# Shift columns in three loads, a quarter of the scale columns accumulated on VectorE, and the last q tile from shifted k-tiles

## Chip, cores, metric

One core of one Trainium2 chip. The metric is device microseconds of one execution. The kernel before takes about 831 us.

## The reference, cut to what matters

A transformer block: a conditioned layer norm, linear attention, a second conditioned layer norm and a gated feed-forward. Only the first projection matters here. The conditioning vector `c` gives one scale (`ca`) and one shift (`sa`) per column; `x` has 2048 rows of 1024 columns.

```python
mod = (_silu(c) @ w_mod).reshape(c.shape[0], 6, 1, -1)
sa, ca, ga, sb, cb, gb = (...)                      # 1024 columns each
h = _layernorm(x, axis=-1) * (1 + ca) + sa
x = x + ga * _A_ref(h, A_wqkv, A_wo)                # q, k, v = h @ wqkv ; linear attention ; @ wo
# [... second half cut ...]
```

## The kernel before

Rows come in four chunks of 512. The first chunk's q projection runs while the weights of scale and shift still arrive. Scale and shift are therefore computed in pieces, each just ahead of the k-tile (128 columns of `h`) that needs it. One piece of 128 columns is eight matmuls with one output column ("products"), into bank 0 of PSUM, the memory that TensorE writes (the program divides it into eight banks):

```python
def mod_sc(w, c0, ms):                       # scale (WCA, c0=8) or shift (WSA, c0=0) columns of the tiles ms
    for m in ms:
        for kt in range(NDT):
            P.pe("matmul", out=PS[:, 0, c0 + m:c0 + m + 1], lhsT=w[:, kt, m * 128:(m + 1) * 128],
                 rhs=SILUC[:, kt:kt + 1], ...)
def fin_ca(m, n):                            # VectorE: 1 + scale, out of bank 0
def fin_sa(m, n, cast=False):                # VectorE: shift, out of bank 0, in float32 and as bf16
```

K-tiles 6 and 7 get scale and shift before use. K-tiles 0 to 5 are used scaled only, and their shift is added to q as a bias, `wq.T @ shift` (`bias_mm`, one-column matmuls again). Seven q tiles accumulate at once in seven banks, k-tile by k-tile; the eighth follows in bank 0. The program orders its work by banks: its recorder of operations makes an access of one engine to a bank wait for the last access of any other engine to it (one such wait is the 0.35 us at 22.30 in the profile after, below).

```python
for nt in range(7):
    if nt == 3:
        mod_sc(WCA, 8, range(4, 8)); fin_ca(4, 4)
        for dt in (4, 5): h0_scale_only(dt)            # VectorE
    q_part(nt, qb[nt], (2, 3))
act_stats(4)
for nt in range(7):
    if nt == 4:
        mod_sc(WSA, 0, range(6, 8)); fin_sa(6, 2)      # needs shift columns 768-1023
        for dt in (6, 7): h0_scale(dt)                 # VectorE, scale and shift
    q_part(nt, qb[nt], (4, 5))
mod_sc(WSA, 0, range(4, 6)); fin_sa(4, 2, True)
for nt in range(7):
    if nt == 2: bias_mm((4, 5))
    q_part(nt, qb[nt], (6,))
for nt in range(7):
    if nt == 1:
        mod_sc(WSA, 0, range(4)); fin_sa(0, 4, True)   # needs shift columns 0-511
        # [... statistics of x tile 5 ...]
    if nt == 4: bias_mm(range(4)); bias_fin()
    q_part(nt, qb[nt], (7,))
# [... eighth q tile in bank 0, then exp and relu of all q tiles, then k of chunk 0 ...]
```

The shift columns come in two loads of 512 columns: 512-1023 ahead of the last two weight tiles, 0-511 behind them.

Of the kernel before, what the change touches and what calls it, by code (L numbers as in the profile page):

```python
# [6 lines left out]
BF16 = mybir.dt.bfloat16  # L7
U8 = mybir.dt.uint8
ACT = mybir.ActivationFunctionType
ALU = mybir.AluOpType  # L10
# [252 lines left out]
def bass_adaLN_cond__linear_attn_block__swiglu_ffn__prompt_kernel(  # L263
# [17 lines left out]
    NDT = D // 128  # L281
# [4 lines left out]
    with ExitStack() as es:  # L286
# [6 lines left out]
        def T(name, off, shape, dt):  # L293
            n = 1
            for s_ in shape[1:]:
                n *= s_
            assert off % 32 == 0 and off + n * mybir.dt.size(dt) <= ARENA, (name, off, shape)
            return nc.alloc_sbuf_tensor_at(name, shape, dt, offset=base + off)
# [3 lines left out]
        PQT = T("pqt", 32 * KB, [128, NHG, S], BF16)  # L302
        WCA = T("wca", 32 * KB, [128, NDT, D], BF16)
        WSA = T("wsa", 48 * KB, [128, NDT, D], BF16)
        AT = T("at", 72 * KB, [128, NFT, 512], BF16)
        SM = 64 * KB
# [7 lines left out]
        MODCOL = T("modcol", SM + 1120, [128, 4, NDT], FP32)  # L314
# [13 lines left out]
        ZCOL = T("zcol", SM + 2304, [128, NHG], FP32)  # L328
        RED = T("red", SM + 2336, [128, NDT], FP32)
        MASK4 = T("mask4", SM + 2368, [128, 4], BF16)  # L330
        BIASQ = T("biasq", SM + 2784, [128, NDT], FP32)
        SUMXH = T("sumxh", SM + 2816, [128, NST, 2], FP32)
        NMR = T("nmr", SM + 2944, [128, NST], FP32)
# [5 lines left out]
        HT = T("ht", 120 * KB, [128, 2, NDT, 512], BF16)  # L339
# [7 lines left out]
        ACC = T("acc", 192 * KB, [128, D], FP32)  # L347
        MHL = T("mhl", 196 * KB, [128, 2, D], BF16)
# [7 lines left out]
        SILUF = T("siluf", SM + 7744, [128, NDT], FP32)  # L356
# [22 lines left out]
        PS = nc.alloc_psum_tensor("ps", [128, 8, 512], FP32)  # L379
# [12 lines left out]
        wmv = w_mod.rearrange("(kt p) n -> p kt n", p=128)  # L392
        cv8 = c.rearrange("o (kt p) -> (o kt) p", p=128)

        P = _Prog()
# [5 lines left out]
        def ca_load(p):  # L401
            P.dma("wca%d" % p, WCA[:, :, 512 * p:512 * p + 512], wmv[:, :, D + 512 * p:D + 512 * p + 512])

        def sa_load(p):
            P.dma("wsa%d" % p, WSA[:, :, 512 * p:512 * p + 512], wmv[:, :, 512 * p:512 * p + 512])

        def wq_load(i, n=1):
            P.dma("wq%d" % i, WQK[:, i:i + n, 0:D], wqkvv[:, i:i + n, 0:D])
# [3 lines left out]
        wq_load(2, 2)  # L412
        ca_load(1)
        wq_load(4, 2)
        sa_load(1)
        wq_load(6)
        wq_load(7)
        sa_load(0)
        for j in range(2):
            P.dma("x1_%d" % j, XRES[:, 4 + j, :], xv[:, 4 + j, :])  # L420
        for i in (1, 0):
# [21 lines left out]
        P.dve("memset", ap=MASK[:], constant=0.0)  # L443
        for h in range(4):
            P.dve("memset", ap=MASK[32 * h:32 * h + 32, 32 * h:32 * h + 32], constant=1.0)
        P.dve("memset", ap=MASK4[:], constant=0.0)
        for h in range(4):
            P.dve("memset", ap=MASK4[32 * h:32 * h + 32, h:h + 1], constant=1.0)
        P.dve("memset", ap=ZSEL[:], constant=0.0)
# [54 lines left out]
        def mod_sc(w, c0, ms):  # L504
# [3 lines that stand above are left out]
                         rhs=SILUC[:, kt:kt + 1], start=mod_first[0], stop=(kt == NDT - 1), skip_group_check=True)  # L508
                    mod_first[0] = False

        def fin_ca(m, n):
            P.dve("tensor_scalar", out=MODCOL[:, 0, m:m + n], in0=PS[:, 0, 8 + m:8 + m + n], scalar1=1.0, scalar2=None,
                  op0=ALU.add)

        def fin_sa(m, n, cast=False):
            if cast:
                P.dve("tensor_copy", out=MODTMP[:, m:m + n], in_=PS[:, 0, m:m + n])
            P.dve("tensor_copy", out=MODCOL[:, 1, m:m + n], in_=PS[:, 0, m:m + n])

        def h0_scale_only(dt):  # L520
            P.dve("tensor_scalar", out=HT[:, 0, dt, :], in0=HT[:, 1, dt, :], scalar1=MODCOL[:, 0, dt:dt + 1],
                  scalar2=None, op0=ALU.mult)

        def h0_shift(dt):
            P.dve("tensor_scalar", out=HT[:, 0, dt, :], in0=HT[:, 0, dt, :], scalar1=MODCOL[:, 1, dt:dt + 1],
                  scalar2=None, op0=ALU.add)

        def bias_mm(dts):
            for nt in range(NDT):
                for dt in dts:  # L530
                    P.pe("matmul", out=PS[:, 0, 16 + nt:17 + nt], lhsT=WQK[:, dt, nt * 128:(nt + 1) * 128],
                         rhs=MODTMP[:, dt:dt + 1], start=False, stop=(dt == 3), skip_group_check=True)

        def bias_fin():
            P.dve("tensor_copy", out=BIASQ[:], in_=PS[:, 0, 16:24])

        def t_view(dt, n=1):
            return PSB[:, 4 + dt // 2, (dt % 2) * 512:(dt % 2 + n) * 512]
# [112 lines left out]
        def phi_evac(bank, dst, bias=0.0):  # L651
            i = phi_ctr[0] % 4
            phi_ctr[0] += 1
            P.act("activation", out=E1[:, i, :], in_=PS[:, bank, :], func=ACT.Exp, bias=bias)
            if not isinstance(dst, tuple):
                P.act("activation", out=RL[:, i, :], in_=PS[:, bank, :], func=ACT.Relu, bias=bias)
            phi_pend.append((i, dst, bank))
            if len(phi_pend) == 2:
                phi_flush()
# [22 lines left out]
        def q_part(nt, bank, dts):  # L682
            for dt in dts:
                P.pe("matmul", out=PS[:, bank, :], lhsT=WQK[:, dt, nt * 128:(nt + 1) * 128],
                     rhs=HT[:, 0, dt, :], start=(dt == 0), stop=(dt == 7))
# [56 lines left out]
        def q_phase_chunk0(side):  # L742
            qb = [1, 2, 3, 4, 6, 7, 5]
            fin_ca(2, 2)
            for dt in (2, 3):
                h0_first(dt, "dve")
            for nts, dts in ((range(4), (0,)), (range(4), (1,)), ((4, 5, 6), (0, 1))):
                for nt in nts:
                    q_part(nt, qb[nt], dts)
            for nt in range(7):  # L750
                if nt == 3:
                    mod_sc(WCA, 8, range(4, 8))
                    fin_ca(4, 4)
                    for dt in (4, 5):
                        h0_scale_only(dt)
                q_part(nt, qb[nt], (2, 3))
            act_stats(4)
            for nt in range(7):
                if nt == 4:
                    mod_sc(WSA, 0, range(6, 8))  # L760
                    fin_sa(6, 2)
                    for dt in (6, 7):
                        h0_scale(dt)
                q_part(nt, qb[nt], (4, 5))
            mod_sc(WSA, 0, range(4, 6))
            fin_sa(4, 2, True)
            for nt in range(7):
                if nt == 2:
                    bias_mm((4, 5))
                q_part(nt, qb[nt], (6,))  # L770
            for nt in range(7):
                if nt == 1:
                    mod_sc(WSA, 0, range(4))
                    fin_sa(0, 4, True)
                    ln_ops[1][0]()
                    ln_ops[1][1]()
                if nt == 4:
                    bias_mm(range(4))
                    bias_fin()
                q_part(nt, qb[nt], (7,))  # L780
            ln_ops[1][2]()
            ln1_rstd1(5)
            for f in act_mv_ops(4):
                f()
            neg_rstd(4)
            q_phi = lambda nt: phi_evac(qb[nt] if nt < 7 else 0, PQT[:, nt, 0:512], bias=BIASQ[:, nt:nt + 1])
            for i, dt in enumerate((4, 5, 0, 1, 2, 3, 6, 7)):
                P.pe("matmul", out=PS[:, 0, :], lhsT=WQK[:, dt, 896:1024], rhs=HT[:, 0, dt, :], start=(i == 0),
                     stop=(i == 7))
            for dt in (4, 5):  # L790
                h0_shift(dt)
            ln1_xn(5)
            th_dma(5)
            for dt in range(4):
                h0_shift(dt)
            ln1_xn(4)
            th_dma(4)
            for nt in range(8):
                q_phi(nt)
                for f in side.get(nt, []):  # L800
                    f()
            qk_ctr[0] = 0
# [5 lines left out]
        ln_ops = [ln1_stats_ops(4 + jj) for jj in range(4)]  # L808
# [291 lines left out]
        for ch in range(NCH):  # L1100
            nxt = ch + 1 if ch + 1 < NCH else None
            for ft in range(NFT):
# [4 lines left out]
                for dt in range(NDT):  # L1107
                    P.pe("matmul", out=PS[:, gbank, :], lhsT=GUG[slot][:, dt, ftl * 128:(ftl + 1) * 128],
                         rhs=H2T[:, dt, :], start=(dt == 0), stop=(dt == NDT - 1))
                for dt in range(NDT):  # L1110
                    P.pe("matmul", out=PS[:, ubank, :], lhsT=GUU[slot][:, dt, ftl * 128:(ftl + 1) * 128],
                         rhs=H2T[:, dt, :], start=(dt == 0), stop=(dt == NDT - 1))
# [4 lines left out]
                if ch == 0 and ft % 2 == 0 and ft < 14:  # L1117
                    i = ft // 2
# [11 lines left out]
                if nxt is None and ft in (8, 12):  # L1130
# [3 lines left out]
                          in1=GB_B[:, 896:1024].unsqueeze(1).to_broadcast([128, f1 - f0, 128]), op=ALU.mult)  # L1134
# [5 lines left out]
            for j in range(4):  # L1140
# [3 lines left out]
                if not last:  # L1144
                    for ft in range(NFT):
                        for nh in range(2):
                            P.pe("matmul", out=PS[:, bb + nh, :], lhsT=AT[:, ft, j * 128:(j + 1) * 128],
                                 rhs=WD(ft)[:, nh * 512:nh * 512 + 512], start=(ft == 0), stop=(ft == NFT - 1))
                for nh in range(2):
                    i = nh  # L1150
                    parts = [(0, 384, bb + 1), (384, 512, 4)] if last and nh == 1 else [(0, 512, bb + nh)]
                    for (c0, c1, pb) in parts:
                        if last:
                            for ft in range(NFT):
                                P.pe("matmul", out=PS[:, pb, c0:c1], lhsT=AT[:, ft, j * 128:(j + 1) * 128],
                                     rhs=WDG[:, ft, :] if c0 > 0 else WD(ft)[:, nh * 512 + c0:nh * 512 + c1],
                                     start=(ft == 0), stop=(ft == NFT - 1))
# [46 lines left out]
```

## Time and profile before

| | before |
|---|---|
| median of the first 3 runs, us | 830.80 (830.74 to 831.32) |
| profiled span, us | 829.4 |
| TensorE busy | 99% of the span |

These lines are from the page of the kernel before: the span, busy time, and the chain of work that ended last, by engine and by line. (All operations are recorded through one helper, hence one line number.)

```profile
span 829.4 us, 10017 instructions
...
PE 823.2 (99%) x4083; PEld 378.8 (46%) x4083; DVE 312.6 (38%) x665; ACT 197.5 (24%) x336; POOL 39.9 (5%) x57
...
PE 97%; DMA 2%; SPq 1%; issue 0%; DVE 0%
PE ps L176 97%; DMA wsa<-in_w_mod_dram 2%; SPq L176 1%; DVE xres L176 0%
```

TensorE bounds the kernel. The chain ends in a load, `wsa`, the shift columns.

This is the TensorE timeline, before: start, length, engine, operation, output<-inputs, count, and in brackets idle time and what ended it. `wca` are products for the scale, `wsa` for the shift, `modtmp` for the bias.

```profile
10.28 0.54 PE L176 MATMUL ps<-siluc,wca 128*128 128x1 bf16 x16
...
16.29 0.94 PE L176 MATMUL ps<-siluc,wca 128*128 128x1 bf16 x32
17.09 3.61 PE L176 MATMUL ps<-ht,wqk 128*128 128x512 bf16 x16
20.93 0.55 PE L176 MATMUL ps<-siluc,wsa 128*128 128x1 bf16 x16 [0.23 <-DMA wsa<-in_w_mod_dram]
21.34 1.46 PE L176 MATMUL ps<-ht,wqk 128*128 128x512 bf16 x6
...
25.30 0.95 PE L176 MATMUL ps<-siluc,wsa 128*128 128x1 bf16 x32
...
26.75 0.94 PE L176 MATMUL ps<-modtmp,wqk 128*128 128x1 bf16 x32
27.56 2.75 PE L176 MATMUL ps<-ht,wqk 128*128 128x512 bf16 x12
```

Two marks are used from here on. **P** is the start of the first scale product (10.28 here). **E** is the end of the last bias product (27.56, where the next matmul starts; some matmul records are missing from a trace, and where that one is, E is the start of the last bias products plus the 0.70 us that 28 of them take elsewhere). From E to the end of the span TensorE hardly waits: 829.4 - 27.56 = 801.8 us, and that remainder was within 0.1 us of 801.8 in 12 of the 18 traces of this study. So the stage from P to E is where the change acts, and its length was 17.28 us.

The weight-load side of TensorE, in the view of waits restricted to 10 to 30 us:

```profile
PEld ps L176 <- DMA wsa<-in_w_mod_dram: 1.1, 2, 0.7
```

(Total, times, longest, in us. Weight loads run ahead of the matmuls, so they show a wait as longer than the array loses by it: the longest here is 0.7, and the array's own wait at 20.93 is 0.23.)

### The profile page before, as it was taken

How to read it: one execution, taken by the hardware profiler on the slowest of the kernel's cores; microseconds unless marked ns; L12 is line 12 of the kernel's file. 1: busy time of each engine (PE TensorE's matmuls, PEld its weight loads, DVE VectorE, ACT ScalarE, POOL GpSimd, SP SyncE). 2: the span in 40 equal slices, each digit the busy share in tenths (PEclk: the TensorE clock that was granted, in tenths of full speed). 3: DMA queues.
4: the chain of work that ended last, by engine and by line, in shares of the span. 5: the costliest groups of instructions: out<-in, count | busy, mean ns of one | idle time of the engine just before them, and what ended most of it. 6: DMA issues, size and time to landing. Idle time of an engine off the chain costs nothing.

```text
span 829.4 us, 10017 instructions
## 1 busy us (share of the span) xinstructions
PE 823.2 (99%) x4083; PEld 378.8 (46%) x4083; DVE 312.6 (38%) x665; ACT 197.5 (24%) x336; POOL 39.9 (5%) x57
## 2 busy tenths in 40 slices
PE   8999999999999999999999999999999999999998
PEld 4544444444444444444444444444444444444444
DVE  5797986756955521121221112122111211221111
ACT  4757641323242111011111101111110111111011
POOL 1010000000130000030000003000000300000000
PEclk9999999999999999999999999999999999999999
DMA  9969656938397985700455571045557004553000
GB/s 321 287 151 231 148 159 171 201 104 304 60 256 229 276 264 158 192 25 15 124 155 150 153 185 33 16 124 153 154 151 190 26 18 123 154 152 87 0 26 26
DMA packets 199246, 119.28 MB, mean 144 GB/s; under 512 B 57881, under 2 KB 182945, under 8 KB 199201
## 3 DMA queue, kind: packets, MB, share of 16 engines
q1 hardware_dynamic: 199184, 118.65, 52.8%
q8 instruction: 32, 0.52, 0.3%
q14 instruction: 14, 0.11, 0.0%
q10 hardware_dynamic: 16, 0.00, 0.0%
HBM read 100.67 MB, written 4.33 MB: 127 GB/s over the span
## 4 chain that ended last, share of the span: by engine, by line
PE 97%; DMA 2%; SPq 1%; issue 0%; DVE 0%
PE ps L176 97%; DMA wsa<-in_w_mod_dram 2%; SPq L176 1%; DVE xres L176 0%
## 5 line engine op out<-in xcount | busy, mean ns | idle before, releaser
L176 PE MATMUL ps<-h2t,gug 128*128 128x512 bf16 x896 | 211.7, 379 | 0.0
L176 PE MATMUL ps<-h2t,guu 128*128 128x512 bf16 x896 | 211.7, 379 | 0.0
L176 DVE TENSOR_TENSOR at<-sg,ps 128x512 bf16<-128x512 bf16 x112 | 77.0, 687 | 282.8 <-PE ps L176 281.2
L176 ACT ACTIVATE sg<-ps 128x512 bf16<-128x512 f32 x112 | 66.9, 597 | 309.7 <-PE ps L176 309.7
L176 PEld LDWEIGHTS ps<-h2t,guu 128*128 128x128 bf16 x896 | 87.6, 98 | 105.7
L176 PEld LDWEIGHTS ps<-h2t,gug 128*128 128x128 bf16 x896 | 87.7, 98 | 105.5
L176 PE MATMUL ps<-wd_a,at 128*128 128x512 bf16 (+1 forms) x512 | 112.4, 377 | 0.0
L176 PE MATMUL ps<-ht,wqk 128*128 128x512 bf16 x512 | 111.7, 379 | 0.0
L176 PE MATMUL ps<-wd_b,at 128*128 128x512 bf16 (+1 forms) x384 | 85.0, 377 | 0.0
L176 PEld LDWEIGHTS ps<-wd_a,at 128*128 128x128 bf16 x512 | 50.1, 98 | 59.6
L176 DVE TENSOR_TENSOR ut<-att,gb_b 128x512 bf16<-128x512 bf16 (+1 forms) x32 | 14.3, 447 | 166.8 <-ACT att L176 166.8
L176 PEld LDWEIGHTS ps<-ht,wqk 128*128 128x128 bf16 x512 | 49.5, 98 | 58.7 <-DVE biasq L176 0.2
L176 ACT ACTIVATE att<-ps 128x512 bf16<-128x512 f32 (+1 forms) x32 | 17.4, 591 | 182.1 <-PE ps L176 182.1
L176 PEld LDWEIGHTS ps<-wd_b,at 128*128 128x128 bf16 x384 | 37.6, 98 | 44.7
L176 PE MATMUL ps<-pk,xres 128*128 128x512 bf16 x256 | 56.5, 379 | 0.0
L176 PE MATMUL ps<-mw,pqt 128*128 128x512 bf16 x256 | 56.3, 379 | 0.0
L176 POOL TENSOR_SCALAR h2t<-h2t,modcol 128x512 bf16<-128x512 bf16 x32 | 26.3, 836 | 383.4 <-DMA h2t<-xn 383.4
L176 ACT ACTIVATE e<-ps 128x512 bf16<-128x512 f32 x56 | 33.1, 603 | 31.7 <-PE ps L176 19.8
L176 PEld LDWEIGHTS ps<-mw,pqt 128*128 128x128 bf16 x256 | 24.9, 98 | 30.2 <-DVE xres L176 0.4
L176 PEld LDWEIGHTS ps<-pk,xres 128*128 128x128 bf16 x256 | 24.9, 98 | 29.9 <-issue 0.4
L176 ACT ACTIVATE junk<-xres 128x1024 bf16<-128x1024 bf16 x24 | 25.4, 1058 | 35.1 <-DVE xres L176 34.9
L176 DVE SCALAR_TENSOR_TENSOR xres<-ps,xres 128x512 bf16<-128x512 f32 x32 | 21.4, 688 | 12.3 <-PE ps L176 11.5
(107 smaller groups left out, 344.8 us busy)
## 6 DMA issues: line engine op xcount, KB each, us to landing
gug<-in_B_w_gate_dram SPq DMA_DIRECT2D x56, 512.0 KB, 4.0
guu<-in_B_w_up_dram SPq DMA_DIRECT2D x56, 512.0 KB, 5.3
xres<-in_A_x_dram SPq DMA_DIRECT2D x20, 256.0 KB, 7.7
rb<-recip_den SPq DMA_DIRECT2D x8, 512.0 KB, 11.5
stgx<-in_w_mod_dram SPq DMA_DIRECT2D x2, 2048.0 KB, 7.9
wd_a<-in_B_w_down_dram SPq DMA_DIRECT2D x4, 1024.0 KB, 7.8
out_dram<-xres SPq DMA_DIRECT2D x31, 128.0 KB, 1.7
xres<-in_A_x_dram SPq DMA_DIRECT2D x3, 1024.0 KB, 14.1
```

The source lines that it names most:

```text
L176: return getattr(e, method)(**kw)
```

## The change

Its intent is to take one-column matmuls off TensorE and to have the shift columns for tiles 6 and 7 earlier:

- the shift load of columns 512-1023 is cut in two, and 768-1023 goes first;
- the scale columns 768-1023 are no longer 16 products: VectorE multiplies and adds the eight k-tiles, splits the float32 sum into two bf16 parts, and 4 products with a column of ones add over the partitions;
- the scalings of k-tiles 4 and 5 go to ScalarE, to free VectorE for that;
- k-tiles 0 to 5 are shifted early, so the eighth q tile needs no bias (7 bias columns instead of 8), and the statistics of x tile 5 go behind the shifts.

```diff
-        sa_load(1)
+        sa_load(768, 1024)
         wq_load(6)
         wq_load(7)
-        sa_load(0)
+        sa_load(512, 768)
+        sa_load(0, 512)
@@
+        def part_macc_ops(w, c0, n):          # [... cut: 2 multiplies, 6 multiply-adds in two accumulators ...]
+            ops.append(lambda: P.dve("tensor_tensor", out=acc[0], in0=acc[0], in1=acc[1], op=ALU.add))
+            ops.append(lambda: P.dve("tensor_copy", out=MHL[:, 0, c0:c0 + n], in_=acc[0]))
+            ops.append(lambda: P.dve("tensor_tensor", out=MHL[:, 1, c0:c0 + n], in0=acc[0], in1=MHL[:, 0, c0:c0 + n],
+                                     op=ALU.subtract))
+        def part_sum(c0, ms):                 # [... 2 products per tile, with ONESC ...]
@@ h0_scale_only
-            P.dve("tensor_scalar", out=HT[:, 0, dt, :], in0=HT[:, 1, dt, :], scalar1=MODCOL[:, 0, dt:dt + 1], ...)
+            P.act("activation", out=HT[:, 0, dt, :], in_=HT[:, 1, dt, :], func=ACT.Copy, scale=MODCOL[:, 0, dt:dt + 1])
@@
                 if nt == 3:
-                    mod_sc(WCA, 8, range(4, 8))
-                    fin_ca(4, 4)
+                    mod_sc(WCA, 8, range(4, 6))
+                    fin_ca(4, 2)
                     for dt in (4, 5):
                         h0_scale_only(dt)
+                    for f in part_macc_ops(WCA, 768, 256):
+                        f()
@@
                 if nt == 4:
+                    part_sum(8, (6, 7))
+                    fin_ca(6, 2)
                     mod_sc(WSA, 0, range(6, 8))
@@
             fin_sa(4, 2, True)
+            for dt in (4, 5):
+                h0_shift(dt)
@@
                     fin_sa(0, 4, True)
-                    ln_ops[1][0]()
-                    ln_ops[1][1]()
+                    for dt in range(4):
+                        h0_shift(dt)
```

Cut: seven bias columns instead of eight, the order of k-tiles in the eighth q tile, the later place of `ln_ops[1]`.

More of the change, by code (lines that the diff above doesn't have):

```diff
@@ L330, in bass_adaLN_cond__linear_attn_block__swiglu_ffn__prompt_kernel @@
         MASK4 = T("mask4", SM + 2368, [128, 4], BF16)
+        ONESC = T("onesc", SM + 2400, [128, 1], BF16)
         BIASQ = T("biasq", SM + 2784, [128, NDT], FP32)
@@ L402, in ca_load, with sa_load @@
             P.dma("wca%d" % p, WCA[:, :, 512 * p:512 * p + 512], wmv[:, :, D + 512 * p:D + 512 * p + 512])
-        def sa_load(p):
-            P.dma("wsa%d" % p, WSA[:, :, 512 * p:512 * p + 512], wmv[:, :, 512 * p:512 * p + 512])
+        def sa_load(c0, c1):
+            P.dma("wsa%d" % c0, WSA[:, :, c0:c1], wmv[:, :, c0:c1])
         def wq_load(i, n=1):
@@ L445, in bass_adaLN_cond__linear_attn_block__swiglu_ffn__prompt_kernel @@
             P.dve("memset", ap=MASK[32 * h:32 * h + 32, 32 * h:32 * h + 32], constant=1.0)
+        P.dve("memset", ap=ONESC[:], constant=1.0)
         P.dve("memset", ap=MASK4[:], constant=0.0)
@@ L518, in fin_sa @@
             P.dve("tensor_copy", out=MODCOL[:, 1, m:m + n], in_=PS[:, 0, m:m + n])
+        def part_macc_ops(w, c0, n):
+            acc = [ACC[:, i * n:(i + 1) * n] for i in range(2)]
+            ops = []
+            for kt in range(NDT):
+                a, src, sc = acc[kt % 2], w[:, kt, c0:c0 + n], SILUF[:, kt:kt + 1]
+                if kt < 2:
+                    ops.append(lambda a=a, src=src, sc=sc: P.dve("tensor_scalar", out=a, in0=src, scalar1=sc,
+                                                                 scalar2=None, op0=ALU.mult))
+                else:
+                    ops.append(lambda a=a, src=src, sc=sc: P.dve("scalar_tensor_tensor", out=a, in0=src, scalar=sc,
+                                                                 in1=a, op0=ALU.mult, op1=ALU.add))
+            ops.append(lambda: P.dve("tensor_tensor", out=acc[0], in0=acc[0], in1=acc[1], op=ALU.add))
+            ops.append(lambda: P.dve("tensor_copy", out=MHL[:, 0, c0:c0 + n], in_=acc[0]))
+            ops.append(lambda: P.dve("tensor_tensor", out=MHL[:, 1, c0:c0 + n], in0=acc[0], in1=MHL[:, 0, c0:c0 + n],
+                                     op=ALU.subtract))
+            return ops
+        def part_sum(c0, ms):
+            for m in ms:
+                for i in range(2):
+                    P.pe("matmul", out=PS[:, 0, c0 + m:c0 + m + 1], lhsT=MHL[:, i, m * 128:(m + 1) * 128],
+                         rhs=ONESC[:], start=False, stop=(i == 1), skip_group_check=True)
         def h0_scale_only(dt):
-            P.dve("tensor_scalar", out=HT[:, 0, dt, :], in0=HT[:, 1, dt, :], scalar1=MODCOL[:, 0, dt:dt + 1],
-                  scalar2=None, op0=ALU.mult)
+            P.act("activation", out=HT[:, 0, dt, :], in_=HT[:, 1, dt, :], func=ACT.Copy,
+                  scale=MODCOL[:, 0, dt:dt + 1])
         def h0_shift(dt):
@@ L528, in bias_mm @@
         def bias_mm(dts):
-            for nt in range(NDT):
+            for nt in range(NDT - 1):
                 for dt in dts:
@@ L534, in bias_fin @@
         def bias_fin():
-            P.dve("tensor_copy", out=BIASQ[:], in_=PS[:, 0, 16:24])
+            P.dve("tensor_copy", out=BIASQ[:, 0:NDT - 1], in_=PS[:, 0, 16:23])
         def t_view(dt, n=1):
@@ L780, in q_phase_chunk0 @@
                 q_part(nt, qb[nt], (7,))
-            ln_ops[1][2]()
+            for f in ln_ops[1]:
+                f()
             ln1_rstd1(5)
@@ L785, in q_phase_chunk0 @@
             neg_rstd(4)
-            q_phi = lambda nt: phi_evac(qb[nt] if nt < 7 else 0, PQT[:, nt, 0:512], bias=BIASQ[:, nt:nt + 1])
-            for i, dt in enumerate((4, 5, 0, 1, 2, 3, 6, 7)):
+            q_phi = lambda nt: phi_evac(qb[nt] if nt < 7 else 0, PQT[:, nt, 0:512],
+                                        bias=BIASQ[:, nt:nt + 1] if nt < 7 else 0.0)
+            for i, dt in enumerate((6, 7, 4, 5, 0, 1, 2, 3)):
                 P.pe("matmul", out=PS[:, 0, :], lhsT=WQK[:, dt, 896:1024], rhs=HT[:, 0, dt, :], start=(i == 0),
                      stop=(i == 7))
-            for dt in (4, 5):
-                h0_shift(dt)
             ln1_xn(5)
             th_dma(5)
-            for dt in range(4):
-                h0_shift(dt)
             ln1_xn(4)
```

## The prediction

> **What bounds the kernel.** TensorE. Busy table: PE 99% of the 829.4 us span, clock row full throughout. The chain that ended last is 97% TensorE: from 20.93 us to 826.8 us it is one unbroken run of matmuls; before that it goes through the load of shift columns 512-1023, landing at 20.88. So only the opening can change, by about 1 us.
>
> Timeline of the opening, in TensorE order: scale products (32) 16.29-17.09; 16 q matmuls (0.217 us each) to 20.56; wait until 20.93 for the shift load (0.23 us in the waits); shift products, 16 in 0.41 us; wait for VectorE 0.1 us; last shift products at 25.30, as their load lands (25.25): nearly no wait; bias products 26.75-27.56. A 128x1 product costs 0.025 us.
>
> **Removed from TensorE.** Scale columns 768-1023: 16 products become 4, minus 0.30 us. Bias of the last q tile: 2+4 products, minus 0.15 us. So 0.45 us, plus the 0.37 us gap at 20.93, since columns 768-1023 of the shift should land 1.5 us earlier (0.52 MB at the 360 GB/s that the windows show), near 19.4. The last shift load has the same bytes ahead of it and lands near 25.3 as before.
>
> **Added.** Eleven VectorE operations on 256 columns, in a row, on which TensorE then waits. The same operations on 1024 columns: multiply-add 1.28 us, first product 0.75, cast 0.68, subtract 1.23. A one-column multiply-add takes 0.21, so about 1.05 ns per column, and 256 columns take about 0.48 (estimate). [...] Independent neighbours overlap by about 0.07 us, dependent ones don't. Estimate: 2x0.28 + 5x0.40 + 0.52 + 0.46 + 0.33 + 0.42 = 4.3 us. They can start only behind the scale columns of tiles 4-5, near 17.0, and end near 21.3. TensorE is ready at 16.69 + 3.47 = 20.2. So it waits 1.1 us where it waited 0.37.
>
> Behind the 4 products TensorE must wait again: VectorE reads bank 0 before TensorE may write there (before: 0.4 us from the last product to VectorE's end, which q matmuls covered; now nothing lies between). Shift products for 6-7 then start near 21.85, not 20.93: 0.9 us late. After that loads come early enough, and the bias products give back 0.15 us. Net about +0.75 us.
>
> The two scalings moved to ScalarE end near 18.6, when their first reader comes: neutral. The earlier shifts push the statistics of x tile 5 back. The second chunk's modulation is ready only about 0.3 us before TensorE needs it (it starts at 42.3); I expect the later TensorE to cover this, with a stall of 0 to 0.3 us as risk.
>
> **Prediction: 831.5 us, 8 in 10 within 830.6 to 832.2.** Faster by over 2%: 0.003; within 2%: 0.994; slower by over 2%: 0.003.
>
> **What would show it.** Right: TensorE idles about 1 us near 20.2-21.3, released by VectorE's split of the accumulated columns, then about 0.4 us released by the scale column; no wait on shift loads; the eleven operations take 4 to 4.6 us; the q stage ends 0.6 to 0.9 us later. Wrong: TensorE reaches the last shift load early and waits for it (time then 830.4 to 830.8), or a new wait at 43-46 us.
>
> **What would make it wrong.** VectorE done in under 3.5 us; the shift loads slower in narrow rows (512 B); a stall at the second chunk beyond 0.3 us.

One sentence is cut from the record under "Added": it put a float32 operation of two tensors on 256 columns at 0.42 us, by a rule that no run of this case shows. The sum came to 4.3 us. Its last term, 0.42, rested on that rule, and probably the 0.46 of the add before it. It can be estimated from the profile of before alone: the same operation takes 1.23 us on 1024 columns there, and 768 columns fewer at the 1.05 ns of the record make 0.42; the add's term would be that and a pause of 0.04.

## The result, and the profile after

| | before | after |
|---|---|---|
| median of 6 runs, us | 830.88 (830.53 to 832.01) | 832.55 (832.14 to 833.15) |
| ratio, 95% interval | | 1.0018 (1.0005 to 1.0031) |
| profiled span, us | 829.4 | 830.5 |
| P, E, E - P in the profile, us | 10.28, 27.56, 17.28 | 10.71, 28.73, 18.02 |
| time less span, us | 1.8 | 2.0 |

A ratio is the mean time of one kernel's fast runs over that of the other's of the same rounds, so it isn't quite the ratio of the medians quoted. The change costs 1.67 us by the medians; 0.7 was predicted over the 830.8 known then (0.75 in the sum), and the range ended at 832.2. The outcome lies above the range.

The same lines of the page, after:

```profile
span 830.5 us, 9998 instructions
...
PE 822.9 (99%) x4065; PEld 378.5 (46%) x4065; DVE 316.7 (38%) x676; ACT 198.6 (24%) x338; POOL 39.7 (5%) x57
...
PE 98%; DVE 1%; DMA 1%; ACT 0%; SPq 0%; issue 0%
PE ps L176 98%; DMA xres<-in_A_x_dram 1%; DVE acc L176 0%; DVE stats L176 0%; ACT xres L176 0%; SPq L176 0%; DVE mhl L176 0%; DVE modcol L176 0%; DVE xres L176 0%; DVE mv L176 0%; DVE nmr L176 0%
```

TensorE's busy time fell by 0.3 us and the span still grew. The chain is another one: it goes back through VectorE's accumulation (`acc`, `mhl`), and through the layer norm of an x tile (`stats`, `nmr`) to that tile's load (`xres`). The load of shift columns is gone from it. The chain in order of time (start, length, what) shows both:

```profile
1.71 4.18 DMA xres<-in_A_x_dram
...
5.91 1.29 DVE stats L176 x2
...
8.72 8.61 PE ps L176 x105
...
17.52 2.91 DVE acc L176 x8
...
21.72 0.25 PE ps L176 x3
...
22.00 0.17 DVE modcol L176
```

The TensorE timeline of the stage, after:

```profile
10.71 0.54 PE L176 MATMUL ps<-siluc,wca 128*128 128x1 bf16 x16
...
16.72 0.54 PE L176 MATMUL ps<-siluc,wca 128*128 128x1 bf16 x16
17.12 3.61 PE L176 MATMUL ps<-ht,wqk 128*128 128x512 bf16 x16
21.26 0.18 PE L176 MATMUL ps<-onesc,mhl 128*128 128x1 bf16 x1 [0.53 <-DVE mhl L176]
21.72 0.23 PE L176 MATMUL ps<-onesc,mhl 128*128 128x1 bf16 x3 [0.28 <-DVE mhl L176]
22.30 0.54 PE L176 MATMUL ps<-siluc,wsa 128*128 128x1 bf16 x16 [0.35 <-DVE modcol L176]
22.70 1.46 PE L176 MATMUL ps<-ht,wqk 128*128 128x512 bf16 x6
...
26.58 0.94 PE L176 MATMUL ps<-siluc,wsa 128*128 128x1 bf16 x32
...
28.02 0.84 PE L176 MATMUL ps<-modtmp,wqk 128*128 128x1 bf16 x28
28.73 1.46 PE L176 MATMUL ps<-ht,wqk 128*128 128x512 bf16 x6
```

And VectorE's timeline, for what TensorE waits for at 21.26, 21.72 and 22.30:

```profile
17.36 0.16 DVE L176 TENSOR_SCALAR modcol<-ps 128x2 f32<-128x2 f32 x1 [3.30 <-PE ps L176]
17.44 0.61 DVE L176 TENSOR_SCALAR acc<-wca,siluf 128x256 f32<-128x256 bf16 x2
...
17.96 2.46 DVE L176 SCALAR_TENSOR_TENSOR acc<-wca,siluf,acc 128x256 f32<-128x256 bf16 x6
...
21.24 0.43 DVE L176 TENSOR_TENSOR mhl<-acc,mhl 128x256 bf16<-128x256 f32 x1
...
22.00 0.16 DVE L176 TENSOR_SCALAR modcol<-ps 128x2 f32<-128x2 f32 x1 [0.33 <-PE ps L176]
```

The view of waits on the weight-load side, 10 to 30 us:

```profile
PEld ps L176 <- DVE mhl L176: 1.4, 2, 1.0
```

The wait for `wsa` is gone. VectorE sat idle for 3.30 us, then ran the eleven operations from 17.44 to 21.67; the weight-load side waited 1.0 us for their first part. Then comes the wait behind the four products, 0.35 us, while VectorE reads bank 0. The shift products for tiles 6 and 7 start at 22.30, which is 11.59 us after P. Before, they started 10.65 us after P. That is the 0.94 us of delay that was predicted (0.9). From there to E it takes 6.43 us instead of 6.63, 0.20 less, most of it the shorter bias, and E - P grows by 0.74. So the stage did what the sum said, and the time grew by twice that. The experiments ask where the rest comes from.

### The profile page after: what moved, and what is told of

Its sections match the earlier page's. It is cut to its first block, busy times and chain, and to the rows that moved or that the text cites. A ratio compares the mean times of both kernels' runs of the same rounds, so it can differ in the third digit from the quotient of the medians.

```text
span 830.5 us, 9998 instructions
## 1 busy us (share of the span) xinstructions
PE 822.9 (99%) x4065; PEld 378.5 (46%) x4065; DVE 316.7 (38%) x676; ACT 198.6 (24%) x338; POOL 39.7 (5%) x57
## 4 chain that ended last, share of the span: by engine, by line
PE 98%; DVE 1%; DMA 1%; ACT 0%; SPq 0%; issue 0%
PE ps L176 98%; DMA xres<-in_A_x_dram 1%; DVE acc L176 0%; DVE stats L176 0%; ACT xres L176 0%; SPq L176 0%; DVE mhl L176 0%; DVE modcol L176 0%; DVE xres L176 0%; DVE mv L176 0%; DVE nmr L176 0%
## 5 line engine op out<-in xcount | busy, mean ns | idle before, releaser
L176 ACT ACTIVATE junk<-xres 128x1024 bf16<-128x1024 bf16 x24 | 25.4, 1059 | 35.1 <-DVE xres L176 34.9
```

The costliest lines, as they stand in the source:

```text
L176: return getattr(e, method)(**kw)
```

## Experiments

All runs have five rounds, beside runs of before on the same chip. "Span" is the median of a kernel's profiled spans. Texts written ahead of the first eight runs call E - P "S".

### Round 1: control, repeat, accumulation out, accumulation early

`aa_before` and `after_again` are the two kernels unchanged.

> The kernel before, unchanged, as its own control. Stage length S = from the first scale product to the end of the last bias product on TensorE (before: 10.28 to 27.56, 17.28 us; after: 10.71 to 28.73, 18.02 us). Theory A (of the 1.7 us, 0.75 is TensorE waiting for VectorE inside S, and the rest is the opening ahead of S, which varies from execution to execution with the arrival of the first x tiles, whatever the kernel): ratio 1.000 within 0.001, S 17.28 within 0.1, but the first scale product may start anywhere from 9.9 to 10.8. Rival B (the change itself delays the opening): first scale product at 10.28 again within 0.1.

> The changed kernel, unchanged, once more beside the control. Theory A: S 18.02 within 0.1; over many executions its opening is as early as before's, so the ratio falls to about 1.0009 (0.75 us) and the first scale product starts anywhere from 9.9 to 10.8. Rival B: first scale product at 10.7 again, ratio 1.0015 to 1.002 again.

| | time, us | span, us | ratio (95%) | P | E | E - P |
|---|---|---|---|---|---|---|
| aa_before | 831.24 | 829.4 | 1.0000 (0.9988 to 1.0013) | 10.08 | 27.34 | 17.26 |
| after_again | 832.81 | 830.8 | 1.0017 (1.0003 to 1.0031) | 10.68 | 28.96 | 18.28 |

`aa_before` met theory A (P 10.08, outside rival B's 10.28 within 0.1). The result repeats: 832.81 against 831.20 for before, and the ratio did not fall to 1.0009, so that part of theory A missed. E - P of the changed kernel was 0.26 us longer than expected; its weight-load side waited for the last shift load, which landed late, at about 26.8. P was late again, so rival B gained.

`products_back`: the changed kernel with its 16 products on TensorE again.

```diff
-                    mod_sc(WCA, 8, range(4, 6))
-                    fin_ca(4, 2)
+                    mod_sc(WCA, 8, range(4, 8))
+                    fin_ca(4, 4)
@@
-                    for f in part_macc_ops(WCA, 768, 256):
-                        f()
@@
-                    part_sum(8, (6, 7))
-                    fin_ca(6, 2)
```

> The changed kernel without its VectorE accumulation: the 16 products for scale columns 768-1023 are back on TensorE; the three shift loads, the two scalings on ScalarE and the last q tile from shifted k-tiles stay. Theory A: both VectorE waits vanish, S falls from 18.02 to 16.8 to 17.2 us (the last shift load sets the floor), time about 0.9 us under the changed kernel and 0.1 to 0.4 us under before. Rival C (the split loads or the ScalarE scalings cost the time, not the accumulation): S stays above 17.7.

Time 832.07, span 830.1, ratio 1.0009 (0.9997 to 1.0022). P 10.44, E 27.58, E - P 17.14, as theory A had it. But the time stayed 0.9 us above before, where theory A had it 0.1 to 0.4 below (a miss, though the interval still holds 1). The span less E is 802.4 instead of 801.8: TensorE meets a new wait, seven times, at the second chunk. The view of waits, 40 to 50 us, of this run:

```profile
PEld ps L176 <- DVE ht L176: 1.6, 7, 0.2
```

Those are the modulated k-tiles of the second chunk, which VectorE makes one by one. The changed kernel has no such line there: it comes 1.2 us later (E 28.73 against 27.58), and VectorE started those k-tiles at 42.82 in it and at 43.12 here, when the transposed tile had landed. This was the prediction's "stall at the second chunk". It suggests that the other parts of the change are not free either.

`macc_early`: the same eleven operations, queued ahead, with the scale of tiles 4 and 5 finished on ScalarE so that it doesn't stand behind them.

```diff
             for dt in (2, 3):
                 h0_first(dt, "dve")
+            for f in part_macc_ops(WCA, 768, 256):
+                f()
@@
-                    fin_ca(4, 2)
+                    P.act("activation", out=MODCOL[:, 0, 4:6], in_=PS[:, 0, 12:14], func=ACT.Identity, bias=1.0)
@@
-                    for f in part_macc_ops(WCA, 768, 256):
-                        f()
```

> The changed kernel with the same eleven VectorE operations queued ahead of the scale fin of tiles 4-5 (that one addition goes to ScalarE), so they start when the second scale load lands (14.9 to 16.3 us) and not behind TensorE's products at 17.4. Theory A: the accumulation ends at 19 to 20.6, TensorE's wait for it falls from about 1.0 to 0 to 0.3 us, the wait behind the four products (0.35 to 0.4 us) stays, S is 16.9 to 17.4. Rival D (the operations or the narrow products cost the time by themselves, wherever they stand): S stays near 18.0.

Time 831.59, span 829.5, ratio 1.0005 (0.9992 to 1.0017); P 10.69, E 27.80, E - P 17.11. In its trace the first of the four products starts at 20.56 with no array wait recorded, and the 0.35 us behind them stays. All five of its runs (831.55 to 831.88) lie under all five of the changed kernel (832.25 to 833.39). So the accumulation cost what it did because of where it stood in VectorE's queue: behind a scale that TensorE produces at 17.1, while the columns that it needs had landed before (time of issue plus time to landing: 14.9 us in the trace of before, 16.3 in that of the changed kernel). Rival D is refuted.

### Round 2: which part moves what

`loads_only` is before with the three loads; `old_loads` is the changed kernel with two. The edit is the load part of the diff above, applied or undone. `bias_only` is before with the last q tile's part of it (the shifts, seven bias columns, the later statistics).

> The kernel before with only the shift columns in three loads (768-1023 first, 512-767 and 0-511 behind the last weight loads). In the four profiles of kernels with the three loads the first scale product so far starts at 10.44 to 10.71, in the two of before at 10.08 and 10.28. Theory B (the split loads delay the opening): first scale product at 10.4 to 10.7, median span of all runs 0.3 to 0.6 us above before's unless the stage gives it back. Theory A (the opening has nothing to do with the loads): 10.0 to 10.4. In both the wait for the first shift columns (0.2 to 0.4 us) goes and comes back at the last shift load, so S is 17.0 to 17.3.

> The changed kernel with the two shift loads of before; all else of the change stays. Theory B: first scale product back at 10.0 to 10.3 and median span 0.3 to 0.6 us under the changed kernel. Theory A: 10.4 to 10.7, span as the changed kernel's (830.5 to 830.8). In both S stays at 18.0, because TensorE waits for VectorE past the landing of the first shift load (20.9).

> The kernel before with only the last q tile reading shifted k-tiles (7 bias columns instead of 8, the shifts earlier on VectorE, the statistics of x tile 5 behind them). S falls by 0.1 to 0.15 us from 17.27. When TensorE was early in the run with the products back on TensorE, it waited about 0.6 us for the second chunk's modulated tiles at 42 to 46 us. Theory E (moving the statistics behind the shifts costs that): TensorE waits 0.2 to 0.7 us there and the time is 0 to 0.5 us above before. Rival (that wait came from the loads): no wait there, time 0.1 us under before.

| | time, us | span, us | ratio (95%) | P | E | E - P |
|---|---|---|---|---|---|---|
| loads_only | 832.43 | 830.6 | 1.0019 (1.0005 to 1.0032) | 10.54 | 28.21 | 17.67 |
| old_loads | 832.59 | 830.6 | 1.0016 (1.0003 to 1.0028) | 10.95 | 28.97 | 18.02 |
| bias_only | 831.38 | 829.6 | 1.0002 (0.9989 to 1.0014) | 10.61 | 27.30 | 16.69 |

Rival B, that the split loads delay the opening, is refuted: with the two loads of before, `old_loads` has the latest opening of all, later than theory A's 10.4 to 10.7 too, and `bias_only` one of 10.61 (`loads_only`'s 10.54 taken alone fell in B's range). What P follows is visible in the traces: the start of VectorE's statistics of the third x tile, which in most of them waits for that tile's load. It is 5.48 us in before, 5.28 in aa_before, 5.91 in after, 5.88 in after_again, 6.15 in old_loads and 5.81 in bias_only, and P is 4.80 us later in every one of them; in eight of the others P is 4.86 to 5.02 us later, and in four of these eight the weight-load side also waits 0.2 us for the scale columns. The load of the third x tile is issued at 1.7 us and its statistics start by 6.15 in these profiles, while the first shift load, the first that the change touches, is issued at 7.8 us or later. Over 17 profiles (all but the one with a deliberate delay) P runs from 10.08 to 10.95, with median 10.61, and kernels with parts of the change stand near both ends (`macc_only` 10.16, `old_loads` 10.95). One doubt stays: the ten kernels with the ScalarE scalings have a median P of 10.68, the seven without 10.39. Nothing of the scalings runs before 17 us, and with one profile for each kernel this can be chance, but no run excludes that some part of the change delays the opening a little.

The row that tells most is `bias_only`. Its P was 0.33 us later than that of before, and its E was 0.26 us earlier. Its TensorE timeline:

```profile
10.61 0.54 PE L176 MATMUL ps<-siluc,wca 128*128 128x1 bf16 x16
...
17.43 3.61 PE L176 MATMUL ps<-ht,wqk 128*128 128x512 bf16 x16
20.88 0.54 PE L176 MATMUL ps<-siluc,wsa 128*128 128x1 bf16 x16
...
25.15 0.94 PE L176 MATMUL ps<-siluc,wsa 128*128 128x1 bf16 x32
...
27.30 2.97 PE L176 MATMUL ps<-ht,wqk 128*128 128x512 bf16 x13
```

No wait for shift loads: it came late enough to find them landed. Its 16.69 us are bare work; with the six bias products that it saves (0.025 us each) before's bare work is 16.84. So 0.44 of before's 17.28 us were waits for loads whose landing P does not set. With an opening as early as 10.28 before has that much slack: the early opening gains it nothing, and a later one costs it nothing until the slack is used up. In the changed kernel nothing in the stage waits for a load (after_again's last one excepted), so E = P + 18.02 and a late opening counts in full, as the timeline of `old_loads` shows, 0.24 us later than after in every line:

```profile
10.95 0.54 PE L176 MATMUL ps<-siluc,wca 128*128 128x1 bf16 x16
...
21.50 0.18 PE L176 MATMUL ps<-onesc,mhl 128*128 128x1 bf16 x1 [0.53 <-DVE mhl L176]
...
28.97 1.24 PE L176 MATMUL ps<-ht,wqk 128*128 128x512 bf16 x5
```

`loads_only` adds a point of its own: E - P is 17.67, not 17.0 to 17.3, with waits of 0.25 and 0.23 us for the second and third shift load. The loads got slower. The view of windows (stretch; us, busy time and count of PE, PEld, DVE, ACT and POOL; granted clock; DMA share; GB/s), first of before, then of the changed kernel:

```profile
17.00:20.00 3.00, 3.00 (x24) 1.46 (x21) 0.78 (x3) 0.00 (x0) 0.00 (x0) 1.00 1.08 363
```

```profile
17.00:20.00 3.00, 3.00 (x25) 1.46 (x22) 2.64 (x9) 1.34 (x2) 0.00 (x0) 1.00 1.09 327
```

The busy share of the DMA engines is about the same and the rate is 10% lower. In this stretch the eleven traces with two loads have 360 to 365 GB/s, the seven with three loads 327 to 332. Rows of 256 columns are 512 bytes; whether it is the narrow rows or the third load that costs was not separated. The last shift load landed (time of issue plus time to landing) at a median of 25.1 us over eleven profiles with two loads (24.4 to 26.5) and 25.6 over seven with three (25.4 to 26.8); the prediction had it at 25.3 either way. So the three loads alone put `loads_only` 1.2 us above before, nearly as far as the whole change does, and they would be a rival for the cause if `old_loads`, without them, were not as slow (832.59) with the same E - P as the changed kernel. Of the 1.2 us, 0.65 is the later E of the one profile (28.21 against 27.56); the rest stays open. That profile also has a wait of 1.5 us at 148 us, for a row that goes to memory and back; what the loads have to do with that was not tried.

`bias_only`'s time, 831.38 against 831.20, lies in its expected 0 to 0.5 us and within the noise. Its two short waits at the second chunk stand in `aa_before` as well, so they are no sign of the moved statistics. A miss was E - P: it fell by 0.58 from the 17.27 expected of before, and not by 0.1 to 0.15, because the waits went too.

`respaced` is the mend that the theory suggests: `macc_early`, two q tiles between the four products and the shift products, the last shift products and their bias later, and the statistics of x tile 5 ahead of the shifts again. (Cut below: the lines of `macc_early`, the shift products of tiles 4 and 5 two q tiles later and their bias three, the later place of the last shifts.)

```diff
                 if nt == 4:
                     part_sum(8, (6, 7))
                     fin_ca(6, 2)
+                if nt == 6:
                     mod_sc(WSA, 0, range(6, 8))
@@
-                if nt == 1:
+                if nt == 3:
                     mod_sc(WSA, 0, range(4))
                     fin_sa(0, 4, True)
-                    for dt in range(4):
-                        h0_shift(dt)
-                if nt == 4:
+                    ln_ops[1][0](); ln_ops[1][1]()
+                if nt == 5:
                     bias_mm(range(4))
                     bias_fin()
```

> The changed kernel mended by the theory: accumulation queued early with the scale fin of tiles 4-5 on ScalarE; two q tiles between the four products and the shift products that must wait for VectorE's read of bank 0; the last shift products two q tiles later; the statistics of x tile 5 ahead of the shifts again. Expected if theories A and E are right: no wait of TensorE over 0.15 us in the stage but on the last shift load, S 16.3 to 16.9, no new wait at 42 to 46 us, time 0.3 to 0.9 us under before if the opening were equal, and about equal to before if the three loads delay the opening by 0.4. If S stays over 17.3, the bank order was not what cost.

Time 832.10, span 830.1, ratio 1.0011 (0.9999 to 1.0024); P 10.47, E 27.75, E - P 17.28: a miss. The wait behind the four products went, but TensorE now waited 0.34 us for VectorE's scaling of tile 6, which had moved too close to its reader. Behind E it lost another 0.5 us (span less E 802.3).

### Round 3: slack, the rest outside the span, a second mend

`before_late`: two memsets on VectorE delay the opening of before.

```diff
+        for _ in range(2):
+            P.dve("memset", ap=RL[:, 0, :], constant=0.0)
         act_xn(0, MV[:, 0, 0:1])
```

> The kernel before with two 128x512 memsets (together about 0.5 us) on VectorE in the opening, ahead of the scaling of the first x tile, so that the first scale product (P) starts later. So far, E being the end of the last bias product: before-like kernels have P 10.08, 10.28, 10.61 and E 27.34, 27.56, 27.30; the changed VectorE chain gives E = P + 18.02 (10.71 and 28.73; 10.95 and 28.97). Theory F (before has slack: TensorE waits for the two shift loads, whose landing doesn't depend on P, so an early opening gains it nothing; with a late opening the waits go and E = P + 16.84, its bare work): here P is 10.6 to 11.3, both waits on shift loads are gone, E - P is 16.8 to 16.95, and the median time rises by only 0.1 to 0.45 us. Rival G (no slack, the opening counts in full): E - P stays 17.25 and the time rises by 0.5 us.

Time 831.61, span 829.8, ratio 1.0011 (0.9999 to 1.0024), against 830.99 and 829.2 of before: up by 0.62 us, which is above theory F's 0.1 to 0.45 and close to rival G's 0.5. The one profile fell on the longest of the five executions (832.1):

```profile
9.96 0.62 PE L176 MATMUL ps<-ident,xres 128*128 128x128 bf16 x8 [2.16 <-ACT xres L176]
10.41 2.23 PE L176 MATMUL ps<-e,ident 128*128 128x512 bf16 x5
...
13.29 0.61 PE L176 MATMUL ps<-siluc,wca 128*128 128x1 bf16 x16
13.76 1.12 PE L176 MATMUL ps<-ident,xres 128*128 128x128 bf16 x16
```

P was 13.29, 3.01 us later than in before, for three reasons. The statistics of the third x tile started 1.09 us later (6.57). The memsets then added 0.58: from those statistics to the first transposes of that tile it took 3.39 us, and 2.81 in before and in the changed kernel. The rest is TensorE at a lower clock (the mean of this run is 0.998): from 10.41 to 13.29 five matmuls of 512 columns and eight transposes take 2.88 us, and 1.53 in before. In this profile the waits for shift loads are gone, as F says, and E - P is 16.98. About 0.14 of that is the lower clock (the two stretches up to 14.72 take 0.47 and 0.96 us, and 0.40 and 0.89 in before), which leaves the 16.84 of bare work. With P that late the waits had to go, so the profile confirms the bare work and not the size of the slack. The times say more of the slack: four of the five executions ran at full clock, and the delay of 0.58 us raised their spans by about 0.6 as well. So in an ordinary execution of before, unlike the one that was profiled, little or no slack is left; this is G's outcome for the time.

The profiles of kernels like before with P from 10.08 to 10.61 have E from 27.29 to 27.56, and with P at 10.77 and 10.81 (`act_scale_only`, `act_bias` below) E is 27.79 and 27.50: no trend with P up to 10.6. (In `ones_bias`, P 10.66, a shift load landed over 1 us late and E is 28.73; landing times vary too.)

The time less the span, 1.8 us in before, was about 2.0 in the changed kernel: 0.2 us lie outside what the profile covers. `ones_only` is before with the added memset, `act_scale_only` before with the scalings on ScalarE. Both edits are single lines of the diff above.

> The kernel before with only the added memset of the column of ones (VectorE, 0.06 us), nothing reads it. Time less span is 1.80 to 1.84 us in before, in the split loads alone and in the bias part alone, but 1.97 to 2.08 in every kernel that holds this memset and the two scalings on ScalarE. If the memset causes that: time less span 2.0 here, time 0.2 us above before. If not: 1.8, and time as before. It also tells whether the memset shifts the opening: first scale product 10.0 to 10.7 if not.

> The kernel before with only the two scalings of k-tiles 4 and 5 moved from VectorE to ScalarE. If these cause the 0.2 us outside the span: time less span 2.0. If not, 1.8. The scalings end near 18.5 to 18.9, when tile 4 is first read; I expect a TensorE wait of 0 to 0.3 us for them, taken back by the wait for the first shift load, so time within 0.2 us of before either way apart from the 0.2 in question.

`ones_only`: 831.01, ratio 1.0003 (0.9990 to 1.0015), P 10.39, E 27.29, time less span 1.81. `act_scale_only`: 831.50, ratio 1.0005 (0.9992 to 1.0017), P 10.77, E 27.79, time less span 1.83. Neither alone makes the 0.2.

`respaced2`: the mend with two loads and the shift products one q tile earlier (`if nt == 5`).

> The mended version with the two loads of before and the shift products of tiles 6-7 one q tile earlier (in the first mend TensorE waited 0.34 us for VectorE's scaling of tile 6). Theory: shift loads land at 20.3 to 20.9 and 24.7 to 25.3 again, 0.7 us earlier at the end than with three loads (25.4 to 26.8); no TensorE wait over 0.2 us between 12 and 30 us; E - P is 16.4 to 16.7 against 16.84 of bare work in before; later a wait of 0 to 0.4 us at the second chunk. Time 0 to 0.4 us under before if time less span stays 1.8, 0.2 more if it is 2.0.

Time 831.35, span 829.4, ratio 1.0004 (0.9990 to 1.0018), against 830.99 and 829.2. P 10.26 and E about 27.0, so E - P is 16.8, a little over what was expected, and time less span is 1.97. It is 1.2 us under the changed kernel's first result and doesn't beat before.

### Round 4: is it VectorE's chain, one for one?

`macc_only` is before with the accumulation alone: column of ones, eleven operations, four products. Loads, scalings and bias stay.

> The kernel before with only the accumulation (column of ones, eleven VectorE operations, 4 products); two shift loads, VectorE scalings and the bias of eight tiles stay. Theory A (VectorE's chain is the gate, and E = P + a constant because nothing in it waits for a load): the two VectorE scalings (0.57 us) now stand ahead of the chain, and 4 + 2 bias products more (0.15) behind it, so E - P is 18.02 + 0.57 + 0.15 = 18.7 within 0.1. If the other parts had a share in the 18.02, E - P is 18.2 or less. Time 1.6 to 2.1 us above before.

Time 833.71, span 831.9, ratio 1.0033 (1.0021 to 1.0046); the three executions with TensorE at full clock took 832.63 to 833.71. P 10.16, E 28.99, E - P 18.83; expected 18.7 within 0.1, so slightly long. The chain starts 7.38 us after P and not 6.73 (after): the two scalings in front of it cost 0.65, not 0.57. The accumulation alone thus makes the whole of the stage's growth and more, and the other parts, the ScalarE scalings above all, take some of it back.

`two_more`: the changed kernel with two more multiply-adds in the chain.

```diff
+            for kt in (6, 7):
+                ops.append(lambda kt=kt: P.dve("scalar_tensor_tensor", out=ACC[:, (kt - 4) * n:(kt - 3) * n],
+                                               in0=w[:, kt, c0:c0 + n], scalar=SILUF[:, kt:kt + 1], in1=acc[kt % 2],
+                                               op0=ALU.mult, op1=ALU.add))
```

> The changed kernel with two more multiply-adds of 256 columns in VectorE's chain, into scratch that nothing reads (0.40 us each). Theory A: E - P rises from 18.02 by 0.8 to 18.8 within 0.1, and the time by 0.8 within 0.3: TensorE waits for the chain one for one. Rival (the chain has slack, something else ends the wait): less than 0.4.

Time 834.58, span 832.6, ratio 1.0035 (1.0021 to 1.0049). Up to the shift products the dose acts as said: they start 12.28 us after P instead of 11.59, 0.69 later (0.80 expected; the add that follows now starts 0.08 us before the operation in front of it ends, and 0.03 behind its end in the profile after). But E - P is 20.10, and the time is 1.8 to 2.0 us above the two results of the changed kernel. (They were run at other times.) Its two executions at full clock took 833.24 and 833.25, which is 0.4 to 0.7 above, about the dose. The windows of the profiled run tell where the others lose more, in the column of the granted clock:

```profile
20.00:23.50 3.50, 1.67 (x25) 0.86 (x23) 2.40 (x7) 0.00 (x0) 0.00 (x0) 1.00 1.12 336
23.50:27.00 3.50, 3.50 (x25) 1.44 (x24) 1.50 (x7) 0.41 (x1) 0.00 (x0) 0.51 1.08 362
```

TensorE was busy less than half of one stretch (1.67 of 3.50 us), and in the next one its granted clock was 0.51. The six q matmuls there take 2.52 us instead of 1.46. Three of this kernel's five runs, two of macc_only's and one each of loads_only's and before_late's have a mean clock of 0.998; no run of the changed kernel has. The idle times recorded ahead of the slow stretch sum to 1.20 + 0.28 + 0.35 = 1.83 us, with only four one-column products between them; in `macc_only`'s profile 1.41 us of the same three waits left the clock at full. That the longer waits bring the lower clock on is inference from these runs; what sets it was not shown.

`ones_bias` and `act_bias` are before with two parts each, for the 0.2 us outside the span.

> The kernel before with the memset of ones and the bias part. Each alone leaves time less span at 1.80 to 1.83 us, but kernels that hold these two and the ScalarE scalings, with or without the accumulation and the three loads, have 1.97 to 2.08. If the pair makes it: 1.95 or more here. If it belongs to the pair of scalings and bias: 1.8 here. Time otherwise within 0.3 us of before.

> The kernel before with the ScalarE scalings and the bias part. If this pair makes the 0.2 us outside the span: time less span 1.95 or more here, 1.8 in the run with ones and bias. If neither pair: it can't be put down to one part. Time otherwise within 0.3 us of before, plus 0 to 0.3 for a wait at the second chunk.

`ones_bias`: 831.22, ratio 1.0006 (0.9993 to 1.0018), time less span 1.83; P 10.66, E 28.73 in a run whose first shift load landed only at about 22.1, a wait of 1.03 us. `act_bias`: 831.70, ratio 1.0007 (0.9995 to 1.0020), time less span 1.94; P 10.81, E 27.50, E - P again 16.69. All kernels with both the ScalarE scalings and the bias part have 1.94 to 2.11, all others 1.79 to 1.83. So the pair goes with most of the 0.2; what it is, the profile can't show, and it stays open.

## Why the prediction was wrong

**Right, by the trace.**
- TensorE bounds the kernel, and the span changed in this stage: E is 1.17 us later in the profiles, and the span 1.1 longer.
- The VectorE chain: 4.3 us was the sum, it ran from 17.44 to 21.67, 4.23 us. The last subtract stood in the sum at 0.42 us and took 0.426. The multiply-add was put at 0.48 us and took 0.476; six of them took 2.46 us, so neighbours overlapped by about 0.08 us.
- The two waits: 1.1 us and 0.4 us were foreseen, the weight-load side waited 1.02 and 0.41.
- The stage, 0.75 us longer: 18.02 - 17.28 = 0.74. `macc_early` and `two_more` show that it is the place and length of VectorE's chain that does it.
- Bias: 0.15 us less work was foreseen. The two groups of bias products take 0.42 and 0.81 us before, 0.36 and 0.71 after: 0.16.

**Wrong: the step "So it waits 1.1 us where it waited 0.37", and with it "Net about +0.75 us".** The new wait was right. The old one, 0.37 us for the shift load at 20.93, was taken as a constant of before that the change removes. It was not. The first shift products start 10.65 and 10.63 us after P in the two profiles of before, whose openings are early (10.28, 10.08), but 10.26 to 10.27 in `ones_only`, `bias_only` and `act_bias` (P 10.39, 10.61, 10.81), where the array loses nothing there. The term is thus anything from 0 to 0.37 with the loads on time (and more where a shift load is late, as in `ones_bias`). With the small wait at the last load, 17.28 held 0.44 us of waits and 16.84 us of work; the changed kernel has 18.02 with any opening. Without those waits the difference of the stages is 18.02 - 16.84 = 1.18 us and not 0.75. That ordinary executions of before mostly lack the waits is inferred, from `before_late` (a delay of 0.58 us cost 0.6) and from kernels with one part changed; both profiles of before itself have them. The spans, which every execution has, agree: less 801.8, the medians put E at 27.4 to 27.6 in before and at 28.7 and 29.0 in the changed kernel, 1.1 to 1.6 apart, which is nearer to 1.18 than to 0.75. That both kernels draw their openings alike is not fully shown (round 2). The prediction quoted the evidence itself, "before that it goes through the load of shift columns". In the profile of before, that chain meant that the work ahead of the load had slack in that execution (the waits in the stage came to 0.44 us). The change replaced that wait by a chain that hangs on the opening, so the early opening that gave the profile of before its slack gives the changed kernel none.

**Wrong: the last shift load "lands near 25.3 as before".** The bytes ahead of it are the same, but with the third load and its 512-byte rows they moved at 327 to 332 GB/s and not at 360 to 365, and it lands 0.5 us later by the medians. In most profiles of the changed kernel TensorE comes later still; in after_again it cost 0.26 us. The prediction had named narrow rows as a risk, and sized it at nothing.

**Not in the sum at all:** 0.2 us outside the profiled span.

Together: in after_again the span grew from 829.4 to 830.8 by 1.4 us, of which about 1.2 is the stage (the 1.18 inferred above), and 0.2 outside the span make the measured 1.6. The remaining 0.2 of the span is not settled run by run; the late shift load of one profile is of that size. The range was too narrow for one more reason: single executions of before differ in span from 828.8 to 830.5, and one profile shows one draw.

**The other risk,** a stall at the second chunk, cost half a microsecond in `products_back` and `act_bias`, where TensorE reached it early (span less E 802.4 and 802.3 instead of 801.8), but also 0.4 in `ones_bias`, where E was as late as in the changed kernel and VectorE started those k-tiles only at 44.06. The changed kernel's profiles have no such wait, as the prediction expected.

## What to carry to other kernels

Before subtracting a stage's length, take its waits out and ask of each what the work in front of it could lose without harm: a wait for a load (0.44 us in the stage here) is slack for everything ahead of that load, in the executions that have it, and a change that puts a compute chain in the load's place takes the slack away. Work moved to an idle engine costs by its place in that engine's queue; here the same eleven operations cost TensorE a 1.0 us wait behind one small operation and almost none ahead of it. Where an effect is a few tenths of a microsecond, look at more than one execution of before, and at kernels with one part changed: here a second profile of before (E - P 17.26) would not have shown that the waits in the stage differ from draw to draw.
